# Gated linear attention followed by a multiplicative FFN: first part's output made transposed, heads joined through DRAM, decays moved to partitions by small transfers

## The chip, the cores and the metric

The kernel runs on one core of one Trainium2 chip. The time is the device time of one execution, in microseconds (us). Beside it stands the span of a profiled execution, which is about 2 us shorter (1.7 to 2.1 in every execution on record), and the mean clock that the throttle granted TensorE. All runs compared here were fast (granted clock 0.92 to 0.96) except one execution that is named where it occurs. One execution of each kernel was profiled, and executions of one kernel differ: those of the kernel before had spans of 675.3 to 680.7 us, and its profile, at 675.4, is one of the quickest. So a difference of a few microseconds between two profiles is not a finding by itself. A ratio is the mean time of one kernel's fast runs over the mean time of the kernel before's fast runs in the same rounds, with a 95% interval; it is therefore not quite the ratio of the medians that are quoted beside it.

## The reference, cut to what matters

```python
# q, k, v, alpha: (4 batches, 8 heads, 768 positions, 48), alpha in 0.8..1.0
for t in range(S):                       # part 1, gated linear attention
    state = alpha[:, :, t, :, None] * state + einsum('bhd,bhe->bhde', k[:, :, t], v[:, :, t])
    y[:, :, t] = einsum('bhd,bhde->bhe', q[:, :, t], state)
x = y.transpose(0, 2, 1, 3).reshape(3072, 384)       # the seam: heads side by side
h = (x @ w1) * (x @ w2) @ w3             # part 2; w1, w2: 384x1024, w3: 1024x1024
out = h @ w_out                          # w_out: 1024x384; the weights come in float64
```

## The kernel before

Part 1 runs in 24 chunks of 128 positions, six to a batch. With l the running sum of log(alpha) counted from the middle of the chunk, k is multiplied by e^-l and q by e^l; the state from one chunk to the next is multiplied by e^(sum of this chunk's second half) times e^(sum of the next chunk's first half). Both factors are needed with the feature on the partition. Before, eight matmuls a chunk (`halves`) make them in that layout.

The weights arrive as raw 64-bit words and are turned into float32 tile by tile (36 tiles) by VectorE, ScalarE and GpSimd. Since part 2 multiplies by w3 @ w_out, all of w3 must be converted and folded before part 2 can finish; and the program puts part 2's pieces between part 1's steps from chunk 9 on. So there are two stages: a first one in which weights are converted beside chunks 0 to 8, and a second one that begins with the first *gate* (the 12 matmuls named `pg`).

```python
def decays(n):
    la = las[n % 2]                                  # log(alpha), padded to 64 columns a head
    nc.scalar.activation(la[:, :, 0:D], st.pop(("a", n)), AF.Ln)
    nc.tensor.matmul(lc[:, 0:DM], csum, la[:, :, 0:D], ...)          # 384 columns
    for j in range(NP):                              # the state's factors: 4 products, 2 columns
        nc.tensor.matmul(lc[:, DM + 2*j:DM + 2*j + 2], la[:, 2*j:2*j + 2, :], halves, ...)
    nc.scalar.activation(e[:, DM:], lc, AF.Exp)
    nc.scalar.activation(e[:, 0:DM], lc[:, 0:DM], AF.Exp, scale=-1.0)
    nc.vector.tensor_mul(qks[n % 2][:, :, :, 0:D], st.pop(("kq", n)), e[:, 0:2*DM]...)
...
def attend(n):                                       # y has positions on partitions
    for j in range(NP):
        nc.tensor.matmul(y[:, 2*j:2*j + 2, :], qkT[:, 1, j, :], Ts[n % 2][:, j], ...)
    for h in range(H):
        nc.tensor.matmul(y[:, h, :], ms[:, h % 2, h // 2, :], vc[:, h, :], ...)
    nc.scalar.copy(x, y.rearrange("p h d -> p (h d)"))

def seam(n):                                         # features to partitions, by transposes
    for kk in range(KM):
        nc.tensor.transpose(tp[:, kk, :], x[:, ds(kk*C, C)], ident)
    nc.vector.tensor_copy(out=st["xT", g][:, :, ds(c*C, C)], in_=tp)
    if c == G - 1:
        queue_ffn(g)                                 # part 2 of three chunks
...
for n in range(N):                                   # between(): one weight task, and from
    load(n + AHEAD); transposed(n); between(n)       # chunk 9 on one task of part 2
    scores(n); decays(n + 1); between(n)
    outer(n); between(n)
    attend(n); advance(n); between(n)
    seam(n); between(n)
```

A program's float32 matmul shows as two instructions in the profile, so eight `halves` are four calls here, and sixteen instructions of `y` are eight calls.

## Time and profile before

| | before |
|---|---|
| time, median | 678.39 us (3 runs), 679.19 us (4 runs with those beside the changed kernel) |
| span of the profiled execution | 675.4 us |
| first weight conversion on VectorE starts | 26.18 us |
| first gate starts on TensorE | 192.41 us |
| from there to the end | 483.0 us |

The prediction below shows the shares of the engines. Two more views matter for what followed. The first is the start, in order of time (start, duration, engine or its queue, line, what; SPq is the queue of SyncE):

```profile
2.73 0.71 SPq L101 DMA_DIRECT2D vc<-in_v_dram  x1
3.48 0.93 SPq L98 DMA_DIRECT2D ac<-in_alpha_dram  x1
...
14.48 1.78 SPq L114 DMA_DIRECT2D raw<-in_moe_w_dram  x3
...
14.86 0.96 DVE L198 TENSOR_TENSOR qk<-kq,e 128x768 f32<-128x768 f32 x1 [0.22 <-DMA kq<-in_k_dram]
...
25.24 0.95 DVE L198 TENSOR_TENSOR qk<-kq,e 128x768 f32<-128x768 f32 x1
...
26.18 0.42 DVE L120 TENSOR_SCALAR mant<-raw 128x512 uint32<-128x512 uint32 x1
...
192.41 0.81 PE L315 MATMUL pg<-xT,w 128*128 128x384 f32 x2
```

SyncE goes straight from chunk 0's last load to chunk 1's first (3.48 us) and reaches the first raw weights at 14.48. VectorE, which takes its work in order, has the products of chunks 1 and 2 (14.86 and 25.24) *ahead* of the first conversion at 26.18. The raw words were there by about 21 us (issued from 14.48 on, 4.5 us to landing at the median), so the first conversion did not wait for them; in VectorE's order it stands behind chunk 2.

The second is the cost of the exponentials and of the product that uses them (line, engine, operation, shapes, count | busy us, mean ns | idle before, and what ended it):

```profile
L198 DVE TENSOR_TENSOR qk<-kq,e 128x768 f32<-128x768 f32 x24 | 23.6, 983 | 9.6 <-ACT e L196 9.1 <-DMA kq<-in_k_dram 0.2
...
L196 ACT ACTIVATE e<-lc 128x384 f32<-128x384 f32 x24 | 11.6, 484 | 0.0
```

Each exponential of 384 columns takes 484 ns, and VectorE's product of 768 columns 983 ns.

### The profile page before, as it was taken

What the parts mean: (1) busy time and instruction counts of PE and PEld (TensorE: products, weight loads), DVE (VectorE), ACT (ScalarE), POOL (GpSimd) and SP (SyncE); (2) the same over time, 40 slices, a digit from 0 to 9 for tenths busy, and PEclk for the clock granted to TensorE, in tenths of its full rate; (3) what the DMA queues carried; (4) which work ended last, traced back from release to release, by engine and by line L of the source; (5) the groups of instructions that cost most, each with busy time, mean ns of one, the idle gap of its engine ahead of it and who ended that gap; (6) DMA issues with size and microseconds to landing.
All of it is one profiled execution on the core that took longest, in us unless ns stands there. A gap on an engine that the chain in (4) does not pass through costs nothing.

```text
span 675.4 us, 7729 instructions
## 1 busy us (share of the span) xinstructions
PE 634.9 (94%) x3096; PEld 431.6 (64%) x3096; DVE 229.4 (34%) x369; ACT 169.9 (25%) x333; POOL 128.9 (19%) x144
## 2 busy tenths in 40 slices
PE   5896686998999999999999999999999999999997
PEld 4775675565766666666666666666666666665554
DVE  4589767698321301312122131121302312110110
ACT  3445555566221112111111121111111101110110
POOL 0376656677200000001000100000000000000000
PEclk9857756897999999999999999999999999999999
DMA  9555556677122112012020210201010000000000
GB/s 192 143 161 160 141 140 177 174 209 174 24 40 42 36 35 59 14 34 71 12 48 23 60 36 13 50 21 36 0 48 1 0 13 24 0 1 23 13 0 35
DMA packets 106596, 41.92 MB, mean 62 GB/s; under 512 B 100800, under 2 KB 100800, under 8 KB 106560
## 3 DMA queue, kind: packets, MB, share of 16 engines
q1 hardware_dynamic: 105024, 36.71, 22.9%
q0 software_dynamic: 1536, 4.72, 1.9%
q8 instruction: 24, 0.39, 0.2%
q14 instruction: 12, 0.10, 0.0%
HBM read 36.70 MB, written 4.72 MB: 61 GB/s over the span
## 4 chain that ended last, share of the span: by engine, by line
PE 70%; issue 16%; DVE 8%; POOL 3%; DMA 1%; ACT 1%; POOLq 0%; DVEq 0%; ACTq 0%
PE pg L315 29%; PE po L325 14%; PE y L266 7%; PE pf L305 4%; PE lc L189 3%; PE sc L220 3%; PE lc L191 3%; PE tp L207 3%; DVE mant L120 3%; POOL w L130 2%; PE y L262 2%; DVE power L129 2%; DVE power L127 1%; DMA raw<-in_moe_w_dram 1%; PE tpx L283 1%
## 5 line engine op out<-in xcount | busy, mean ns | idle before, releaser
L315 PE MATMUL pg<-xT,w 128*128 128x384 f32 x768 | 259.9, 490 | 0.0
L315 PEld LDWEIGHTS pg<-xT,w 128*128 128x128 f32 x768 | 141.5, 190 | 87.6
L325 PE MATMUL po<-w3o,ab 128*128 128x384 f32 x384 | 127.7, 488 | 0.0
L318 DVE TENSOR_TENSOR ab<-a,pg 128x384 f32<-128x384 f32 x64 | 35.5, 555 | 242.0 <-PE pg L315 236.6
L325 PEld LDWEIGHTS po<-w3o,ab 128*128 128x128 f32 x384 | 71.6, 190 | 46.2
L317 ACT COPY a<-pg 128x384 f32<-128x384 f32 x64 | 30.7, 479 | 157.4 <-PE pg L315 157.4
L266 PE MATMUL y<-vc,ms 128*128 128x48 f32 x384 | 57.6, 308 | 13.4 <-DVE ms L223 13.3
L253 POOL TENSOR_TENSOR T<-tmp,dec 64x192 f32<-64x192 f32 x40 | 21.6, 540 | 240.3 <-DVE tmp L241 173.7
L266 PEld LDWEIGHTS y<-vc,ms 128*128 128x128 f32 x384 | 55.6, 226 | 16.4 <-DVE ms L223 14.6
L328 POOL DMA_DIRECT2D out_dram<-o x24 | 13.5, 561 | 251.0 <-ACT o L327 251.0
L124 POOL TENSOR_TENSOR mant<-mant,rest 128x512 f32<-128x512 f32 (+1 forms) x36 | 48.3, 1340 | 22.2 <-ACT mant L121 21.7
L305 PE MATMUL pf<-wo,w3T 128*128 128x384 f32 x128 | 46.4, 517 | 0.4 <-DVE w3T L302 0.4
L327 ACT COPY o<-po 128x384 f32<-128x384 f32 x24 | 11.5, 479 | 122.8 <-PE po L325 122.8
L223 DVE TENSOR_TENSOR ms<-sc,keep 128x512 int32<-128x512 int32 x48 | 31.1, 683 | 32.8 <-PE sc L220 32.8
L130 POOL TENSOR_TENSOR w<-mant,power 128x512 f32<-128x512 f32 x28 | 37.1, 1325 | 19.9 <-DVE power L129 19.2
L284 DVE COPY xT<-tpx 128x384 f32<-128x384 f32 x24 | 13.3, 555 | 69.7 <-PE tpx L283 66.4
L305 PEld LDWEIGHTS pf<-wo,w3T 128*128 128x128 f32 x128 | 25.3, 204 | 17.6 <-issue 3.1
L189 PE MATMUL lc<-la,csum 128*128 128x384 f32 x48 | 27.2, 656 | 9.9 <-DVE csum L165 5.6
L120 DVE TENSOR_SCALAR mant<-raw 128x512 uint32<-128x512 uint32 (+1 forms) x36 | 33.2, 923 | 6.8 <-POOL w L130 6.3
L220 PEld LDWEIGHTS sc<-qkT 48*128 48x128 f32 x384 | 25.9, 201 | 12.3 <-issue 9.8
L220 PE MATMUL sc<-qkT 48*128 48x128 f32 x384 | 31.3, 301 | 1.9 <-DVE qkT L211 1.1
L207 PEld LDWEIGHTS tp<-ident,qk 128*128 128x128 f32 x192 | 27.7, 167 | 7.9 <-issue 5.1
(50 smaller groups left out, 492.3 us busy)
## 6 DMA issues: line engine op xcount, KB each, us to landing
raw<-in_moe_w_dram SPq DMA_DIRECT2D x28, 512.0 KB, 4.5
ac<-in_alpha_dram SPq DMA_DIRECT2D x24, 192.0 KB, 3.7
kq<-in_k_dram SPq DMA_DIRECT2D x24, 192.0 KB, 3.6
kq<-in_q_dram SPq DMA_DIRECT2D x24, 192.0 KB, 3.5
vc<-in_v_dram SPq DMA_DIRECT2D x24, 192.0 KB, 2.9
out_dram<-o POOLq DMA_DIRECT2D x24, 192.0 KB, 2.2
raw<-in_moe_w_out_dram SPq DMA_DIRECT2D x8, 384.0 KB, 3.1
```

The lines of the kernel that those rows point to most:

```text
L120: nc.vector.tensor_scalar(top, high, 0x000FFFFF, 0x00100000, op0=ALU.bitwise_and, op1=ALU.bitwise_or)
L124: nc.gpsimd.tensor_add(mant, mant, rest)
L130: nc.gpsimd.tensor_mul(dst, mant, power.bitcast(FP32))
L189: nc.tensor.matmul(lc[:, 0:DM], csum, la[:, :, 0:D], start=True, stop=False, skip_group_check=True)
L207: nc.tensor.transpose(tp[:, j, :], qk[:, i, 2 * j:2 * j + 2, :], ident)
L220: nc.tensor.matmul(sc[i][:, j, :], qkT[r, 0, j, :], qkT[r, 1, j, :], start=True, stop=True)
L223: nc.vector.tensor_tensor(ms[:, i].bitcast(I32), sc[i].bitcast(I32), keep_bc, op=ALU.bitwise_and)
L266: nc.tensor.matmul(y[:, h, :], ms[:, h % 2, h // 2, :], vc[:, h, :], start=first, stop=(h == H - 1), skip_group_check=True)
L305: nc.tensor.matmul(po, w3T[:, j, :], wo[:, j, :], start=(j == 0), stop=(j == KF - 1))
L315: nc.tensor.matmul(p, w[:, kk, ds(f * C, C)], xT[:, kk, :], start=(kk == 0), stop=(kk == KM - 1))
L318: nc.vector.tensor_mul(st["ab", g][:, f, :], a, pb)
L325: nc.tensor.matmul(po, ab[:, f, ds(c * C, C)], w3o[:, f, :], start=(f == 0), stop=(f == KF - 1))
```

## The change

It has three parts. (a) Part 1's output is produced with features on partitions, so that no transposes are needed; v and the state become the stationary operand (the one that is loaded into the array as weights), padded to 64 columns a head. As the padding would remain between the heads, x goes to a DRAM scratch and comes back without it. (b) The `halves` matmuls go. The factors are read out of rows of e, which is on chip already, by transfers that scatter a row over the partitions in pieces of 16 bytes (four values, one of each head pair), from ScalarE's queue, up to four a chunk. To let these rows be read in such pieces, e is laid out with the head pair innermost, so ScalarE writes it and VectorE reads it with a stride of 16 bytes. (c) The exponent at row 0 lacks alpha's first row, so the first rows of all chunks are collected once, at the start, by 32 transfers of 288 single values each (`a0`).

```diff
 # constants, ahead of the loads of chunks 1 and 2
+    with nc.allow_non_contiguous_dma(reason="single values to partitions"):
+        for b in range(B):
+            first = alpha[b].rearrange("(j i) (c s) d -> i d c j s", i=2, s=C)
+            for i in range(2):
+                for j in range(NP):
+                    nc.sync.dma_start(out=a0[ds(DP * i, D), b, :, j], in_=first[i, :, :, j, 0])
     for n in range(1, AHEAD):
         load(n)
 # decays
-        for j in range(NP):
-            nc.tensor.matmul(lc[:, DM + 2 * j:DM + 2 * j + 2], la[:, 2 * j:2 * j + 2, :], halves, ...)
-        e = work.tile([C, 2 * DM + 2 * NP], FP32, name="e", bufs=3)
-        nc.scalar.activation(e[:, DM:], lc, AF.Exp)
-        nc.scalar.activation(e[:, 0:DM], lc[:, 0:DM], AF.Exp, scale=-1.0)
+        e = work.tile([C, 2, 2, D, NP], FP32, name="e")
+        for m, sign in enumerate((-1.0, 1.0)):
+            nc.scalar.activation(e[:, m].rearrange("p i d j -> p j i d"),
+                                 lc.rearrange("p (j i d) -> p j i d", i=2, d=D), AF.Exp, scale=sign)
+            ...
+                for i in range(2):
+                    nc.scalar.dma_start(out=decs[n % 3][ds(DP * i, D), m, :], in_=e[ds(row, 1), i0, i])
-        nc.vector.tensor_mul(...)                    # one product of 768 columns
+        for m in range(2):
+            nc.vector.tensor_mul(...)                # two of 384, reading e with its stride
 # advance
-        nc.vector.tensor_mul(dec, mh[0][:, :, 1:2], mh[1][:, :, 0:1])
+        nc.gpsimd.tensor_mul(dec, decs[(n + 1) % 3][:, 0, :], a0[:, b, c, :])
+        nc.gpsimd.tensor_mul(dec, dec, decs[n % 3][:, 1, :])
 # attend
-                nc.tensor.matmul(y[:, 2 * j:2 * j + 2, :], qkT[:, 1, j, :], Ts[n % 2][:, j], ...)
-            nc.tensor.matmul(y[:, h, :], ms[:, h % 2, h // 2, :], vc[:, h, :], ...)
+                nc.tensor.matmul(y[:, j, :], Ts[n % 2][:, j].rearrange("p i d -> p (i d)"), qkT[:, 1, j, :], ...)
+                nc.tensor.matmul(y[ds(DP * i, DP), j, :], vc[:, 2 * j + i, :], ms[:, i, j, :], ...)
+        for i in range(2):
+            nc.scalar.dma_start(out=to[i, :, :, ds(c * C, C)], in_=x[ds(DP * i, D)])
 # seam: three transposes and a copy a chunk go
+        nc.sync.dma_start(out=st["xT", g], in_=st.pop(("xd", g)).rearrange("(k p) t -> p k t", p=C))
```

## The prediction

> **What bounds the kernel now.** I read the busy shares first (TensorE 94%, VectorE 34%), then the 40 slices:
>
> ```profile
> PE   5896686998999999999999999999999999999997
> DVE  4589767698321301312122131121302312110110
> PEclk9857756897999999999999999999999999999999
> DMA  9555556677122112012020210201010000000000
> ```
>
> A slice is 17 us. There are two stages. For ten slices (170 us) TensorE has gaps and a granted clock of about 0.75, while VectorE and the DMA engines are busy; then TensorE is full at full clock to the end. The table of stretches gives both in numbers (columns: TensorE, weight loads, VectorE, ScalarE, GpSimd, clock, DMA share, GB/s):
>
> ```profile
> 0.00:170.00 170.00, 134.34 (x723) 105.04 (x724) 127.33 (x186) 89.23 (x164) 100.25 (x93) 0.75 0.65 166
> 170.00:676.00 506.00, 500.55 (x2375) 326.52 (x2373) 102.06 (x183) 80.63 (x169) 28.69 (x52) 1.00 0.11 27
> ```
>
> So in the second stage each TensorE microsecond counts in full. TensorE's last wait (3.04 us, for a converted w3 tile) ends at 160.9 us; after it lie three folds of w3, chunks 9 to 23 of part 1 and all of part 2.
>
> The first stage is the weight conversion: 36 tiles, the first at 26.2 us, the last two at 168.7 (VectorE) and 171 us (GpSimd), about 4 us a tile. VectorE is busy 127 of 145 us there, partly because it is held up by GpSimd. The same VectorE instruction, twice:
>
> ```profile
> 155.32 0.42 DVE L127 TENSOR_SCALAR power<-raw 128x512 uint32<-128x512 uint32 x1
> 159.64 1.49 DVE L127 TENSOR_SCALAR power<-raw 128x512 uint32<-128x512 uint32 x1
> ```
>
> It takes 0.42 us beside an idle GpSimd and 1.49 us while GpSimd adds (159.51 to 160.84). The two engines nearly take turns.
>
> Last, one chunk in TensorE's order of time, second stage (start, duration, line):
>
> ```profile
> 223.68 1.16 PE L220 MATMUL sc<-qkT 48*128 48x128 f32 x16
> 224.77 0.91 PE L189 MATMUL lc<-la,csum 128*128 128x384 f32 x2
> 225.52 0.95 PE L191 MATMUL lc<-halves,la 128*128 128x2 f32 x8
> 226.33 4.12 PE L315 MATMUL pg<-xT,w 128*128 128x384 f32 x12
> 230.38 0.67 PE L233 MATMUL s<-vc,qk 128*64 128x48 f32 x16
> 230.98 4.14 PE L315 MATMUL pg<-xT,w 128*128 128x384 f32 x12
> 234.95 1.03 PE L262 MATMUL y<-T,qkT 128*128 128x96 f32 x8
> 235.82 1.91 PE L266 MATMUL y<-vc,ms 128*128 128x48 f32 x16
> 237.56 5.39 PE L325 MATMUL po<-w3o,ab 128*128 128x384 f32 x16
> 242.79 0.49 PE L283 MATMUL tpx<-ident,x 128*128 128x128 f32 x3
> 243.12 5.33 PE L325 MATMUL po<-w3o,ab 128*128 128x384 f32 x16
> ```
>
> Matmuls overlap at their ends, so I count from start to next start: sc 1.09, lc 0.75, halves 0.81, s 0.60, state product 0.87, y 1.74, tpx 0.33, eight transposes tp 0.88 (248.28 to 249.16): 7.07 us a chunk. A gate of 12 matmuls is 4.05, 338 ns each, 0.88 ns a column.
>
> **What the Trainium skill says.** "TensorE: Matmul & The Clock Gate", section LDWEIGHTS: loading time goes by the stationary operand's columns (columns/1.2 ns, so 107 ns for 128), not by what is streamed. The trace agrees: halves streams 2 columns yet takes 0.81/8 = 101 ns, and y with 48 columns 1.74/16 = 109 ns. Both are pure weight loading.
> "TensorEngine Tiling (Array Packing)", Key Properties: different tiles of the array can load and multiply in parallel. The trace agrees in part: s has 64-column weights in two halves of the array and takes 37.5 ns an instruction, under the 48 x 0.88 = 42 of its streaming alone; sc in two row halves takes 68 ns where 128 columns in full would take 113.
> "SBUF — State Buffer", section "SBUF: two separate sides": VectorE and GpSimd share a port pair under an exclusive lock. The 0.42 and 1.49 us above agree.
> "DMA: Bandwidth & Descriptors", Specifications: under 512 B a transfer does a read-modify-write and misses line rate. Here a load of 1024 runs of 192 B goes out about every 0.94 us while the DMA is saturated (7.01 to 10.76 us, four loads); over 16 engines that is 15 ns a run. No row of before shows runs of 4 or 16 B.
>
> **The change, part by part.**
>
> (1) Sums for the state on TensorE (halves) vanish: 8 x 101 ns = 0.81 us a chunk.
>
> (2) Output transposed: y now has v as 64-column weights in two column halves and streams 128 columns, 16 instructions as before. Fully parallel it is 57 ns, in turn 113; I take sc's 68: 16 x 68 = 1.09 for 1.74, a gain of 0.65. The state product streams 128 columns, not 96: 113 or the 109 of loading, so 0.90 for 0.87, a loss of 0.03.
>
> (3) The three transposes of the seam vanish: 0.33. lc reads a tile without gaps and may fall from 375 to 338 ns, a gain of 0.07.
>
> Sum 0.81 + 0.65 - 0.03 + 0.33 + 0.07 = 1.83 us a chunk. The instruction order shows part 2 starting at the same place, in chunk 9, so 15 chunks gain on the path: 15 x 1.83 = 27.5 us.
>
> (4) The detour through DRAM: two stores a chunk, one load a group. There is always work of an older group in front of a group's first gate, even for the last one (in before, x of the last chunk is copied at 604.5 us and the last group's first gate starts at 624.0, after three projections), so a few microseconds of transfers are hidden: 0.
>
> (5) ScalarE issues the small transfers, up to six a chunk. Issues cost SyncE 0.33 to 0.43 us when nothing holds them up, so 2 to 2.6 us of ScalarE a chunk. In the second stage (ScalarE busy 16%) a gate's copy comes at most about 1 us late, which the other PSUM tile's 2.03 us of matmuls covers: 1 us in all. In the first stage the conversion's own ScalarE steps lie behind them; from 8 or 9 chunks x 2.4 = 20 us of issues I let a fifth reach the path: 4 us.
>
> (6) VectorE in the first stage loses xT<-tpx (six copies, 3.3 us, and the 9.2 us it stood waiting for them) and dec (0.9 us); qk is split, which costs about 0.13 x 7. Of these 12.5 us I book 10 as gain, as GpSimd, with 2 us more small products, takes up the rest.
>
> (7) New at the start: 32 transfers of 288 single values stand on SyncE's queue after chunk 0's loads and ahead of chunks 1 to 3 and all weights. They start once VectorE has cleared their target (4.5 us) and need at least 32 x 0.43 = 14 us to issue; 18 values per engine at 15 ns would be 0.27 us each, hidden under the issue, but single values may well be slower. Chunk 1's alpha then lands at 22 us instead of 7, the first raw weight (after 12 more loads of 0.94) at about 34. Chunk 0's work fills only part of it. The first conversion moves from 26.2 to about 37: 11 us lost, 25 if a value costs several times as much.
>
> Sum: 675.4 - 27.5 + 1 + 4 - 10 + 11 = 653.9 us of span; the time lies 3.0 above the span (678.4 against 675.4): 657. TensorE's gains in the first nine chunks, at half clock, also stand on its chain of waits (y alone 13% of the first 175 us); I allow 2 us for them and say **655 us**.
>
> **Rivals.** First, the start becomes the bound: single values at several times 15 ns give 675 or more. For it speaks that SyncE's queue is in order, against it that issue, not data, seems to be the cost of small transfers. Second, the two column halves don't overlap: y stays at 1.8 us, the gain falls to 1.1 us a chunk, and the time is 666. The 37.5 ns of s speak against it, weakly. Third, ScalarE becomes the first stage's bound through its issues, since its busy 89 of 170 us don't count them: 10 to 15 us more, 667. Fourth, the first stage gains more than I book (lc, y and tpx all stand on its chain), giving 640.
>
> **Range and chances.** The second stage's gain is between 16 and 30 us, the first stage's net between -12 and +20. That makes 638 to 674. Faster by over 2% means under 664.8: all rivals but the fourth end above it, the central sum is 10 below. 0.74 faster, 0.23 within 2%, 0.03 slower.
>
> **What would show it.** In the profile after: no halves, no tpx; y near 68 ns an instruction start to start (57 to 113 decides the second rival); a full TensorE row from about slice 10 or 11; SyncE's 32 issues ending near 19 us and the first conversion near 37 us (later: the first rival); VectorE no longer waiting for tpx, and ScalarE's waits in the conversion (the third). I am wrong if the full stage begins much later than 175 us or if gates begin to wait for ScalarE's copies.

## The result, and the profile after

The changed kernel is correct. It took 672.21 us (median of 4 runs, 669.35 to 672.87) against 679.19 for the kernel before; the ratio is 0.9887 [0.9855, 0.9919]. That is 1.1% less: within the predicted range, but not the 3.5% less of its central figure, nor the more than 2% that it held most likely.

The busy shares in 40 slices of the changed kernel (a slice is 16.8 us) and its two stretches, with the columns that the prediction explains:

```profile
PE   3472535498799999999999999999999999999997
...
DVE  3159776877842330231222213303303222110110
```

```profile
0.00:170.00 170.00, 94.31 (x535) 65.41 (x536) 112.22 (x157) 83.56 (x144) 90.23 (x95) 0.76 0.67 161
170.00:671.00 501.00, 491.44 (x2300) 306.98 (x2298) 118.82 (x192) 104.93 (x190) 49.23 (x93) 0.99 0.20 48
```

TensorE is as full as before in the second stage, but in the first 170 us it executes 535 matmul instructions where before it executed 723; some of that difference is the removed ones. VectorE has done 112 us of work in the same window, not 127. To see whether there is more work or later work, one has to count up to the first gate of each kernel: VectorE is then busy for 135 us against 133 before, GpSimd for 109 against 103, ScalarE for 102 against 95 (its transfer issues not counted). That is 2 to 8 us an engine for a gate that is 21.5 us later (below), so most of the delay is work that comes *later*. The first two slices of VectorE (3, 1 against 4, 5) show it.

One chunk in TensorE's order, second stage, to be laid beside that of the prediction:

```profile
242.92 1.16 PE L232 MATMUL sc<-qkT 48*128 48x128 f32 x16
244.01 0.91 PE L195 MATMUL lc<-la,csum 128*128 128x384 f32 x2
244.76 4.03 PE L327 MATMUL pg<-xT,w 128*128 128x384 f32 x12
248.72 0.67 PE L245 MATMUL s<-v,qk 128*64 128x48 f32 x16
249.33 4.14 PE L327 MATMUL pg<-xT,w 128*128 128x384 f32 x12
253.30 1.05 PE L277 MATMUL y<-qkT,T 128*128 128x128 f32 x8
254.28 1.09 PE L281 MATMUL y<-ms,v 128*64 128x128 f32 x16
255.31 0.91 PE L337 MATMUL po<-w3o,ab 128*128 128x384 f32 x2
```

From start to next start: sc 1.09, lc 0.75, s 0.61, state product 0.98, y 1.03, that is 64 ns an instruction. Against the kernel before a chunk gains 0.81 (halves) + 0.71 (y) - 0.11 (state product) + 0.33 (transposes) = 1.74 us, over 15 chunks 26.1 us. From the first gate to the end the profile has 456.6 us where before it had 483.0: 26.4 us less. The second stage gave what was promised.

The start and the first gate, as they were shown of the kernel before:

```profile
4.31 17.83 SPq L181 DMA_DIRECT2D a<-in_alpha_dram  x32
...
12.42 1.23 ACTq L207 DMA_DIRECT2D dec<-e  x2
13.70 0.58 ACT L221 COPY qkT<-tp 128x512 f32<-128x512 f32 x1 [5.76 <-issue]
...
22.18 0.46 SPq L99 DMA_DIRECT2D ac<-in_alpha_dram  x1
...
29.59 1.61 DVE L210 TENSOR_TENSOR qk<-kq,e 128x384 f32<-128x384 f32 x2 [11.86 <-ACT e L199]
...
35.47 6.35 SPq L115 DMA_DIRECT2D raw<-in_moe_w_dram  x3
...
38.74 1.62 DVE L210 TENSOR_TENSOR qk<-kq,e 128x384 f32<-128x384 f32 x2 [1.22 <-ACT e L199]
...
45.40 0.42 DVE L121 TENSOR_SCALAR mant<-raw 128x512 uint32<-128x512 uint32 x1
...
213.88 4.04 PE L327 MATMUL pg<-xT,w 128*128 128x384 f32 x12
```

The 32 transfers hold SyncE's queue from 4.31 to 22.14 us. Chunk 1's alpha goes out at 22.18, 18.7 us later than before. Everything behind it moves: chunk 1's product from 14.86 to 29.59, chunk 2's from 25.24 to 38.74, the raw weights from 14.48 to 35.47, the first conversion from 26.18 to 45.40 (19.2 us later), the first gate from 192.41 to 213.88 (21.5 us later). From the first conversion to the first gate it is 166.2 us before and 168.5 after: the conversion stage itself is hardly longer, it starts later. The line of the `qkT` copy shows a second effect: ScalarE stood 5.76 us, as its first small transfer was not issued before 12.42, 4.5 us after the exponentials. (The profile names one of the 32 transfers as what the copy waited for.)

The account closes: first gate +21.5, rest -26.4, sum -4.9 us, and the spans are 675.4 and 670.5. The medians differ by 7.0 us, 2.1 more, as the profiled execution of the kernel before is a quick one and that of the changed kernel is not.

The same two groups as before:

```profile
L210 DVE TENSOR_TENSOR qk<-kq,e 128x384 f32<-128x384 f32 x48 | 45.2, 984 | 23.1 <-ACT e L199 23.1
L199 ACT ACTIVATE e<-lc 128x384 f32<-128x384 f32 x48 | 37.7, 885 | 48.9 <-PE lc L195 48.9
```

The exponential over 384 columns now takes 885 ns instead of 484, and VectorE's product over 384 columns as long as the one over 768 did. The cause that suggests itself is the 16-byte stride, which an experiment below takes away; the prediction had only 0.13 us a chunk for "qk is split".

### The profile page after: what moved, and what is told of

Its sections match the earlier page's. It is cut to its first block, busy times and chain, and to the rows that moved or that the text cites. A ratio compares the mean times of both kernels' runs of the same rounds, so it can differ in the third digit from the quotient of the medians.

```text
span 670.5 us, 7537 instructions
## 1 busy us (share of the span) xinstructions
PE 585.8 (87%) x2832; PEld 372.4 (56%) x2832; DVE 231.0 (34%) x348; ACT 188.5 (28%) x333; POOL 139.5 (21%) x188
## 3 DMA queue, kind: packets, MB, share of 16 engines
q1 hardware_dynamic: 117952, 41.47, 26.4%
## 4 chain that ended last, share of the span: by engine, by line
PE 62%; issue 17%; DVE 7%; POOL 5%; DMA 4%; ACT 3%; ACTq 0%; SPq 0%; POOLq 0%; DVEq 0%
PE pg L327 28%; PE po L337 14%; PE pf L317 4%; DVE mant L121 3%; PE sc L232 3%; PE y L281 3%; POOL w L131 3%; PE tp L219 2%; PE lc L195 2%; PE y L277 2%; DMA a<-in_alpha_dram 2%; PE s L245 2%; DVE power L130 2%; DMA dec<-e 1%; DVE power L128 1%
## 5 line engine op out<-in xcount | busy, mean ns | idle before, releaser
L330 DVE TENSOR_TENSOR ab<-a,pg 128x384 f32<-128x384 f32 x64 | 35.5, 554 | 249.4 <-PE pg L327 239.0
L232 PE MATMUL sc<-qkT 48*128 48x128 f32 x384 | 34.4, 324 | 24.2 <-ACT qkT L221 19.3
L261 POOL TENSOR_TENSOR dec<-dec,a 128x4 f32<-128x4 f32 x20 | 5.1, 255 | 237.2 <-DMA dec<-e 206.2
L210 DVE TENSOR_TENSOR qk<-kq,e 128x384 f32<-128x384 f32 x48 | 45.2, 984 | 23.1 <-ACT e L199 23.1
L199 ACT ACTIVATE e<-lc 128x384 f32<-128x384 f32 x48 | 37.7, 885 | 48.9 <-PE lc L195 48.9
L232 PEld LDWEIGHTS sc<-qkT 48*128 48x128 f32 x384 | 28.7, 221 | 36.0 <-ACT qkT L221 21.4
L219 PE MATMUL tp<-ident,qk 128*128 128x128 f32 x192 | 31.1, 309 | 12.6 <-DVE qk L210 12.6
L223 DVE COPY qkT<-tp 128x512 f32<-128x512 f32 x24 | 16.6, 690 | 65.9 <-PE tp L219 65.9
L281 PE MATMUL y<-ms,v 128*64 128x128 f32 x384 | 33.4, 300 | 6.5 <-DVE ms L235 6.5
L219 PEld LDWEIGHTS tp<-ident,qk 128*128 128x128 f32 x192 | 25.4, 159 | 21.0 <-issue 12.4
```

The costliest lines, as they stand in the source:

```text
L199: nc.scalar.activation(e[:, m].rearrange("p i d j -> p j i d"), lc.rearrange("p (j i d) -> p j i d", i=2, d=D), AF.Exp, scale=sign)
L210: nc.vector.tensor_mul(qks[n % 2][:, m, :, 0:D].rearrange("p (j i) d -> p j i d", i=2), kq[:, m].rearrange("p (j i) d -> p j i d", i=2), e ...
L219: nc.tensor.transpose(tp[:, j, :], qk[:, i, 2 * j:2 * j + 2, :], ident)
L232: nc.tensor.matmul(sc[i][:, j, :], qkT[r, 0, j, :], qkT[r, 1, j, :], start=True, stop=True)
L281: nc.tensor.matmul(y[ds(DP * i, DP), j, :], vc[:, 2 * j + i, :], ms[:, i, j, :], start=(not inter and j == 0), stop=(j == NP - 1), skip_gr ...
L330: nc.vector.tensor_mul(st["ab", g][:, f, :], a, pb)
```

## The experiments

The second stage came out as computed, so all experiments ask one thing: **what makes the first gate 21.5 us later?** The theory after reading the traces had three terms: the block of 32 transfers at the start (T1), the decays' transfers on ScalarE's queue (T2) and the stride of e (T3). The rivals: the start is harmless and the conversion itself is slowed, by contention or for want of buffers (R1); the transfers cost by their single values, not by their number (R2); the cost is the wait until the values land, not the issue (R3). All times are medians of four runs (of the three fast ones for late10_cvt3); the last three columns are read from the profiled execution.

| run | result | time, us | ratio to before | first conversion | first gate | gate to end |
|---|---|---|---|---|---|---|
| before | correct | 678 to 680 | 1 | 26.2 | 192.4 | 483.0 |
| after | correct | 672.21 | 0.9887 [0.9855, 0.9919] | 45.4 | 213.9 | 456.6 |
| no_a0 | wrong | 652.63 | 0.9596 [0.9561, 0.9631] | 25.3 | 195.3 | 456.5 |
| no_a0_no_dec | wrong | 645.62 | 0.9498 [0.9456, 0.9540] | 24.2 | 187.0 | 456.6 |
| no_a0_no_dec_contig_e | wrong | 642.68 | 0.9449 [0.9417, 0.9482] | 22.0 | 183.6 | 456.6 |
| a0_12dmas | correct | 656.15 | 0.9644 [0.9605, 0.9683] | 35.6 | 198.7 | 456.6 |
| tr_only | correct | 660.29 | 0.9724 [0.9691, 0.9757] | 22.6 | 190.3 | 469.1 |
| sc_only | correct | 681.21 | 1.0028 [0.9989, 1.0067] | 46.4 | 211.1 | 470.0 |
| a0_half | wrong | 666.94 | 0.9826 [0.9794, 0.9858] | 41.6 | 208.2 | 456.6 |
| row_mul | correct | 656.61 | 0.9678 [0.9644, 0.9711] | 24.7 | 197.9 | 456.7 |
| late10 | correct | 651.65 | 0.9580 [0.9546, 0.9614] | 30.3 | 193.7 | 456.5 |
| before_cvt3 | correct | 681.39 | 1.0013 [0.9971, 1.0055] | 27.3 | 193.8 | 483.0 |
| after_cvt3 | correct | 666.93 | 0.9804 [0.9769, 0.9838] | 44.8 | 209.8 | 456.6 |
| dec_unread | wrong | 651.52 | 0.9563 [0.9520, 0.9607] | 24.8 | 193.4 | 456.6 |
| late10_decsync | correct | 657.32 | 0.9673 [0.9633, 0.9712] | 32.3 | 199.0 | 456.5 |
| late10_decpool | correct | 663.51 | 0.9757 [0.9702, 0.9811] | 28.9 | 198.9 | 462.5 |
| late10_cvt3 | correct | 649.06 | 0.9548 [0.9501, 0.9595] | – | – | – |

"Wrong" means that a factor was replaced by 1, so the kernel does the same work on the engines minus the suspected part, and its result is not the reference's. The column "gate to end" is the quiet control: in every variant of the full change but one it is 456.5 to 456.7.

### Three parts taken away one after the other

**no_a0** drops the block at the start (T1):

```diff
-    for x in qks + Ts + decs + [a0]: ...memset(x, 0.0)
-    (the 32 transfers into a0)
+    for x in qks + Ts + decs: ...memset(x, 0.0)
+    nc.vector.memset(a0, 1.0)
```

> The 32 transfers of single values at the start are left out and their target set to 1 (a wrong result on purpose); all else as changed. Theory A (the start is the largest loss: the full stage began 19 to 21 us late because the first conversion moved from 26.2 to 45.4 us): the first conversion comes back to about 28 us, the first gate from 213.9 to about 197, and the time falls from 672 to 653-657. Rival (the conversion stage's own pace sets the end of the stage and takes up an earlier start): 665 or more.

```profile
195.31 4.04 PE L322 MATMUL pg<-xT,w 128*128 128x384 f32 x12
```

The first gate came at 195.3 instead of 213.9, 18.6 us earlier, and the time fell by 19.6. The first conversion is back at 25.3. T1 holds and is the largest term. How much of a delay reaches the gate depends on its size, though, as two runs below show.

**no_a0_no_dec** drops the decays' transfers as well (T2):

```diff
-            nc.scalar.dma_start(out=decs[n % 3][ds(DP * i, D), m, :], in_=e[ds(row, 1), i0, i])
+    for x in decs: nc.vector.memset(x, 1.0)          # once, among the constants
```

> Besides the 32 transfers of the start, the small transfers of the decays from ScalarE's queue are left out too (decays set to 1, a wrong result on purpose); the exponentials still write with a stride. Theory B (layout): these issues cost the path at most 4 us, so 650 to 655, that is within 5 us of the run without the start's transfers. Rival C (ScalarE's issues hold up the conversion): 10 us or more below that run, 643 to 646.

The first gate came 8.3 us earlier still (187.0), the time 7.0 lower. That is more than Theory B's 4 to 5 us and less than Rival C's 10: the issues cost twice what was booked.

**no_a0_no_dec_contig_e** writes e without the stride too (T3):

```diff
-        e = work.tile([C, 2, 2, D, NP], FP32, name="e")
+        e = work.tile([C, 2, NP, 2, D], FP32, name="e")
```

> As the run without any small transfers, but the exponentials are written and read without a stride (wrong result on purpose). Theory B: exponentials fall from 885 to about 490 ns, the products qk from 984 to about 490 ns, and VectorE's about 10 us in the conversion stage come back: 6 to 10 us below the run with the stride, about 643. Rival: the stride's time lies beside other work, within 2 us of the strided run.

The first gate came 3.4 us earlier (183.6), the time 2.9 lower. Its groups show the engines' side, to be laid beside those of the changed kernel:

```profile
L200 DVE TENSOR_TENSOR qk<-kq,e 128x384 f32<-128x384 f32 x48 | 33.3, 730 | 8.3 <-ACT e L196 7.0
L196 ACT ACTIVATE e<-lc 128x384 f32<-128x384 f32 x48 | 21.2, 487 | 41.7 <-PE lc L192 41.6
```

The expected 6 to 10 us did not come. The exponentials are back at 487 ns, as expected; the products' mean only falls from 984 to 730. Their median falls from 859 to 557, however: the mean contains the products that took up to 1658 ns during the conversion. 48 exponentials at 885 ns cost ScalarE some 19 us more in the whole execution than at 487 (48 x 0.398), yet only 3.4 us of first gate come back: most of it lies beside other work. This is the point where the Trainium skill could have warned: "SBUF — State Buffer", Specifications, says that SBUF is read and written in 16-byte lines and that at least two accesses to a line are needed for full bandwidth. A stride of 16 bytes gives each line one. This trace agrees, with 885 against 487 ns.

After the three steps the first gate is at 183.6, 8.8 us earlier than before (192.4). So the sum is 18.6 + 8.3 + 3.4 - 8.8 = 21.5. It closes by construction, as the parts were taken away one after the other; in another order the terms could come out differently. Each of these edits also lets the compiler's scheduler order instructions a little differently, so a term is good to some microseconds, not to tenths.

**Why the layout can't simply be undone:** with e contiguous, the row scatter of 16-byte pieces becomes one of single 4-byte values. By the author's account such a kernel did not build, and neither did one that joins the two transfers of a row into one. No log of these builds is kept, and neither ran.

### The same values in fewer transfers

**a0_12dmas** keeps all 9216 values and results, in 12 transfers of 768 instead of 32 of 288:

```diff
+        first = alpha.rearrange("b (j i) (c s) d -> i c d (b j) s", i=2, s=C)
+        for i in range(2):
+            for c in range(NCH):
+                nc.sync.dma_start(out=a0[ds(DP * i, D), c]..., in_=first[i, c, :, :, 0])
```

> A correct kernel: the same 9216 single values at the start in 12 transfers of 768 instead of 32 of 288. If the cost is the issue (0.56 us each in the changed kernel), the block of issues and values ends after about 7 us instead of 17.8, chunk 1's alpha lands 10 us earlier, and the time is about 662. If the cost is the values (17.8 us over 576 values per DMA engine is 31 ns each), the data still take about 17.8 us, chunk 1's alpha lands at about 26 us as before, and the time stays at 670 to 673.

SyncE's queue in this run, and the first load behind the block:

```profile
4.31 7.79 SPq L180 DMA_DIRECT2D a<-in_alpha_dram  x12
12.14 0.80 SPq L99 DMA_DIRECT2D ac<-in_alpha_dram  x1
```

The block is 7.79 us instead of 17.83, the time 656.15, lower than the expected 662: correct, and 2.4% below the kernel after by the medians. Against no_a0 the first conversion comes 10.3 us later, but the first gate only 3.4. So a block of 8 us costs little at the gate and the 10 us more of the 32 transfers cost 15.2; why the first part is absorbed was not tested. The Trainium skill, "DMA: Bandwidth & Descriptors", Rules for kernel authors, tells to coalesce many small transfers into one; this pair of runs agrees and gives it a size, 10 us of queue for 20 transfers fewer. **a0_half** does the converse: the 32 transfers stay, each with half the values (`b, 0:3, j`).

> The changed kernel with all 32 transfers at the start, but each brings half of the values (144 instead of 288; the other half stays at 1, a wrong result on purpose). If the number of transfers costs (issue[...]), the block stays near 17 us and the time within 3 us of 672. If the values cost, the block falls to about 9 to 15 us (the floor is the issue) and the time falls by 5 us or more.

```profile
4.31 15.61 SPq L182 DMA_DIRECT2D a<-in_alpha_dram  x32
```

Half the values took 2.2 us off the block (17.83 to 15.61), fewer transfers for all the values took 10.0 off it. Number outweighs values in the block. But the time fell by 5.3 us, more than the expected 3, and the first gate came 5.7 us earlier: by the block the run sides with the number, by the time with the values. R2 falls as the main cause and stays as a smaller part.

The block can be split further with the trace: the issues last 0.456 us each at the median, 32 x 0.456 = 14.6 us, and 3.2 us of the block are gaps between them. With half the values a transfer lands 2.7 us after its issue instead of 3.6 (medians), and the gaps shrink to 15.61 - 32 x 0.435 = 1.7 us. So the gaps go with the landing; what makes an issue wait for an earlier landing is not shown by any run. ScalarE's first small transfer depends on the block as well, but only in part: it goes out 4.5 us after the exponentials in the changed kernel and 2.1 us after them in no_a0, which has no block.

### Each half of the change alone

**tr_only** is the kernel before with only the transposed output and the DRAM detour (the new `attend` and `seam`, padded v and T); decays still by `halves`. **sc_only** is the converse: the changed kernel with the old `attend` and `seam`.

> Only the transposed output with the join through DRAM; the decays as before, with eight matmuls a chunk; correct. Theory A (the loss is in the decays' half of the change): from the first gate to the end 456.6 + 15 x 0.81 = 469 us; the first gate comes somewhat before that of the kernel before (192.4) as VectorE no longer waits for the seam, at 183 to 190; time 654 to 662. Rival D (the transposed output itself, its copies and stores, slows the first stage): first gate after 195, time 667 or more.

> Only the decays by small transfers; output and seam as before; correct. Theory A: from the first gate to the end 483.0 - 15 x 0.81 = 471 us; the first gate later than before by the start's 17 to 19 us and by the strided exponentials and products, at 208 to 218; time 681 to 691, slower than before. Rival D: the decays' half is neutral or a gain, time 672 or less.

The second stage split as computed: tr_only's gate to end is 469.1, 13.9 us less than before, sc_only's 470.0, 13.0 less. Their sum, 26.9, is the 26.4 of both together within half a microsecond. The DRAM detour is hidden. In the first stage, sc_only's first gate is 18.7 us later than before and tr_only's 2.1 earlier. Tr_only is inside its expected time (654 to 662) with a first gate at the edge of what was expected (183 to 190). So tr_only gains 2.8% alone; sc_only is the same as before (its interval includes 1), not shown to be slower as its expectation had it. Added up, they would give a first gate at 192.4 + 18.7 - 2.1 = 209.0, but with both it is at 213.9; in medians, tr_only is 18.3 us below its before, sc_only 2.7 above, both together 7.0 below, some 9 us worse than the sum. Both put transfers on ScalarE's queue and both shift the instruction order; which of the two makes the 5 to 9 us is not settled.

### Is it the buffers (R1)?

**before_cvt3** and **after_cvt3** give the conversion a third set of buffers (`cvt = pool("cvt", 3)`, and `outp = pool("outp", 1)` to make room).

> The kernel before with three buffers instead of two for the weights' conversion (and one output buffer instead of three, to make room); correct. Theory P (the conversion stage is paced by the time a tile takes through VectorE, ScalarE and GpSimd with two tiles under way, not by VectorE's busy time): the stage shortens by 10 us or more, time 668 or less. Rival V (VectorE and GpSimd taking turns are the pace): within 4 us of 678.

> The changed kernel with three buffers for the conversion (one output buffer): correct. Theory P: as the path now has ScalarE's issues in the tile's way, a third buffer gains more here than in the kernel before: 12 us or more, 660 or less. Rival V: within 4 us of 672.

Before, nothing came of it (1.0013), as Rival V had it. After, it gave 5.3 us, with the first gate 4.1 us earlier: neither the 12 us of Theory P nor the nothing of Rival V. So buffers did not set the pace in the kernel before, and in the changed kernel a third set buys back a part of the loss. R1 is not the main cause: its first half, a harmless start, is refuted by no_a0, and the stage from the first conversion to the first gate is only 2.3 us longer than before (168.5 for 166.2). Contention by itself was not tested.

### Issue or wait (R3)?

**dec_unread** is no_a0 with the decays' transfers still issued, but with constants used in their place:

```diff
-        nc.gpsimd.tensor_mul(dec, decs[(n + 1) % 3][:, 0, :], a0[:, b, c, :])
-        nc.gpsimd.tensor_mul(dec, dec, decs[n % 3][:, 1, :])
+        nc.gpsimd.tensor_mul(dec, a0[:, (b + 1) % B, c, :], a0[:, b, c, :])
+        nc.gpsimd.tensor_mul(dec, dec, a0[:, b, 0, :])
```

> As the run without the start's transfers (652.6), with the small transfers of the decays issued on ScalarE but never read (GpSimd multiplies constants in their place; wrong result on purpose). If ScalarE's issues cost the 7 us by which leaving the transfers out was faster, it stays at 650 to 654. If it is GpSimd's wait for the values to land, it falls to 645 to 648.

The first gate is at 193.4, against 195.3 with the values read and 187.0 with no transfers. So of the 8.3 us some 6.4 stay with the transfers merely issued. The other 1.9 would be the wait for landing, but that is not shown: the medians of the times are 1.1 us apart (651.52 and 652.63) and the intervals overlap. R3 falls as the main cause of T2. The changed kernel's own row for these issues (min/median/max in ns):

```profile
L207 ACTq DMA_DIRECT2D dec<-e x80: 508/572/1271, 12.4 to 567.1; - x80
```

34 of the 80 are issued before the first gate: 34 x 0.572 = 19 us of ScalarE's queue, of which a third to a half reached the path.

### Versions meant to beat both

**late10** keeps all of the change, merges the start's transfers and puts them behind the loads of chunks 1 and 2. The first chunk of a batch needs none, so ten remain:

```diff
     for n in range(1, AHEAD):
         load(n)
+        for c in range(1, NCH):
+            for i in range(2):
+                nc.sync.dma_start(out=a0[ds(DP * i, D), c]..., in_=first[i, c, :, :, 0])
```

> A correct kernel: the start's values in 10 transfers (the first chunk of a batch needs none), placed after the loads of chunks 1 and 2 instead of before them. If it is the delay of chunk 1's loads and of the weights behind the small transfers that costs, the block of 10 (about 6.5 us) now delays the weights by at most 6 us and chunk 1 not at all: first gate 196 to 199, time 652 to 656, at or below the 12 transfers at the front (656.2). If the number alone counts and not the place, it stays at 656.

```profile
11.24 8.16 SPq L182 DMA_DIRECT2D a<-in_alpha_dram  x10
```

It is correct and takes 651.65 us, 4.2% below the kernel before and 3.1% below the kernel after (by the medians). The block lasts 8.16 us, hardly less than the 7.79 of twelve ahead of the loads, but now it delays only the weights: the first conversion is at 30.3 and the first gate at 193.7, 5.0 us earlier than with a0_12dmas. As the blocks are about equally long, that is the place's doing rather than the two transfers fewer. Place and number are both worth something. The gate is even no later than in no_a0 (195.3), which has no such transfers and converts 5 us earlier: within the few microseconds of scatter nothing of the delay is left.

**row_mul** needs no a0 at all: it multiplies row 0 of e by row 0 of alpha on chip, and keeps a small strided copy `er` of just the rows that are scattered, with e contiguous.

```diff
+        er = work.tile([C, 2, D, NP], FP32, name="er")
+        nc.vector.tensor_mul(er[0:1]..., e[0:1, 0], ac[0:1]...)             # one partition
+        nc.scalar.activation(er[96:C]..., lc[96:C]..., AF.Exp)              # 32 partitions
```

> A correct kernel meant to beat both: no transfers at the start, as row 0 of the chunk's exponentials is multiplied by row 0 of alpha on VectorE before it is scattered; exponentials and products without a stride, only the rows that are scattered are written with one. First gate 185 to 191 and 456.6 us from there: 643 to 650. If the transposed layout's stride and the start are not the causes, it stays above 655.

It missed: 656.61, no better than a0_12dmas. By its own expectation, over 655 would speak against the stride and the start as causes; but the edit also adds work, and no_a0 and no_a0_no_dec_contig_e take these two away without adding any. The likely reason, which no run isolates, stands in one row:

```profile
L196 DVE TENSOR_TENSOR er<-e,ac 1x384 f32<-1x384 f32 x20 | 19.6, 979 | 4.9 <-ACT e L194 3.1 <-DMA xd<-x 0.7
```

A strided product on one partition took 979 ns in the mean, as long as the strided one on 128 partitions (984); the medians are 850 and 859. Making the strided piece narrow saved nothing: nine of these products, 10.2 us of VectorE, and ten strided exponentials, 8.7 us of ScalarE, lie ahead of the first gate.

**late10_decsync** and **late10_decpool** take the decays' transfers off ScalarE and issue them from SyncE or GpSimd.

> Correct; as the best so far (10 late transfers, 651.7), with the decays' transfers issued from SyncE instead of ScalarE. If the place in ScalarE's queue costs, 645 to 648, unless SyncE, which must then wait for each chunk's exponentials before it goes on to the next weights, gives it back. If the transfers as such cost, 650 to 653.

> Correct; the decays' transfers issued from GpSimd. If ScalarE's place costs and GpSimd's own issues (0.56 us each for the output's transfers, four a chunk) cost less: 646 to 650. GpSimd is one of the two engines that take turns in the conversion, so 2.2 us a chunk there should cost as much or more: 651 to 660.

Both are worse than late10, by 5.7 and 11.9 us, and worse than any figure expected of them. ScalarE is the cheapest of the three places in this kernel. With GpSimd the time from the first gate to the end also grew, to 462.5. The trace shows where: TensorE needs 451.8 us from the first gate to its last product in both, and what follows that product lasts 10.7 us instead of 4.7. Why the end is longer is open.

**late10_cvt3** adds the third set of conversion buffers to late10.

> Correct; the best so far with three conversion buffers (one output buffer). If the third buffer covers ScalarE's issues in the tile's way, it gains the same 4 to 6 us as in the changed kernel: 646 to 648. If it only helped with the backlog after the late start, nothing: 650 to 653.

Its three fast executions have a median of 649.06 us; the fourth, the profiled one, was slow (888.53 us at a clock of 0.645), so no profile of it is used. Its interval [0.9501, 0.9595] overlaps that of late10; it is not shown to be better.

## Why the prediction was right or wrong

- **Second stage, parts (1) to (3): right.** 26.4 us measured for 27.5. Of the terms, y gave 0.71 for 0.65 (64 ns an instruction for the assumed 68), the state product cost 0.11 for 0.03 (122 ns for 113), and lc gained nothing where 0.07 was booked.
- **Part (4), the DRAM detour at 0: right.** The time after the first gate is 456.6 with and without every other piece, and tr_only, which has the detour, gave its computed 13.9.
- **Second rival, no column overlap: refuted** by the 64 ns; in turn it would have been 113.
- **Part (6), VectorE freed by 10 us:** the rest of the change, with the three costs taken away, brings the first gate 8.8 us forward. The sum fits; that it comes from VectorE's freed time is not shown. Tr_only frees VectorE of the same copies and waits, and brings the gate only 2.1 us forward, but it keeps `halves` and adds two issues a chunk to ScalarE. And 4.2 of the 8.8 are there already at the first conversion (22.0 for 26.2).
- **Part (7), the start: the step that failed.** The prediction put it as "The first conversion moves from 26.2 to about 37: 11 us lost". It was 45.4, and taking the block away gave 18.6 us. The block itself was sized fairly well (17.8 us for "at least" 14); the first raw load went out at 35.5, so its words were there at about 39.5 (4.0 us to landing at the median) where the prediction had 34. That was not what held the first conversion, which follows chunk 2's masking on VectorE (44.79) without a gap. The error is the step after it: 37 is the prediction's landing of the raw words plus 3 us, as if chunk 1's and 2's work could be done during the wait. But their alpha stands behind the same 32 transfers, and in VectorE's order their products stand ahead of the first conversion: 11.7 us from the first raw load's issue to the first conversion before, 9.9 after. In the changed kernel the delay of the queue (18.7 us at chunk 1's alpha) went through nearly whole; a block of 8 us would not have (a0_12dmas). The prediction's own sign of being wrong, a full stage that begins much later than 175 us, came: the first gate is at 213.9. The mechanism was the first rival's; its cause is not single values that are slow, as that rival had it, but their number and who stands behind them.
- **Part (5), ScalarE's issues: mis-sized.** A fifth of 20 us was allowed to reach the path, 4 us; the issues were 19 us in the first nine chunks as reckoned, but 8.3 came back when they were taken away. The third rival named this, with 10 to 15 us; it was worth more than its place in the sum and less than the rival said.
- **A term was missing: the stride of e,** 3.4 us. It stood in the diff.
- **The sum.** Predicted for the first stage +11 + 4 - 10 = +5, measured 18.6 + 8.3 + 3.4 - 8.8 = +21.5: 16.5 us too little. For the second stage 27.5 and 1 of delay predicted, 26.4 measured. That carries 653.9 to 670.5 of span. That the total fits so well is no test of the single terms, as those of the first stage were measured as a sequence that closes by construction. The chance of "within 2%" at 0.23 was too low, because the range allowed up to +20 for the first stage's net while the chances were set as if +5 were its middle by evidence; no row of the profile before gave the cost of a small transfer.
- **Slips that changed little.** The range does not follow from its parts: a second-stage gain of 16 to 30 us and a net of -12 to +20 in the first give 675.4 - 30 - 12 + 3 = 636 to 675.4 - 16 + 20 + 3 = 682 us, not 638 to 674. The 3.0 us from span to time compare a profiled execution with the median of others; within an execution it is 1.7 to 2.1. TensorE's clock in the first stage is 0.75 in the prediction's own table, not half. And what GpSimd does from 159.51 to 160.84 is a product (L130), not an addition.

## What to carry to other kernels

In this kernel a small transfer cost its issue and its place in an in-order queue, so count the transfers and ask who stands behind them: merged to ten and put behind the loads that start the pipeline, the same values cost nothing that these profiles can tell from scatter, instead of 18.6 us. The saving on the engine that was full came back to the microsecond and could be computed from start-to-start times (26.4 us for 26.1). In the stage where several engines take turns it could not: a first conversion 20.1 us later moved the first gate by 18.6 us, one 10.3 us later by only 3.4. So a delay there has to be measured. Look at each new access pattern's stride as well as at its count of elements; a strided operation didn't get cheaper by using fewer partitions.

## What the Trainium skill lacked or had wrong

- "DMA: Bandwidth & Descriptors", section "Issuing engines are not separate DMA queues", calls the sequencer's time to initiate a DMA "usually small relative to the DMA itself". For a single transfer that agrees: 0.456 us an issue on SyncE, 3.1 to 4.1 us from issue to landing. What the sentence leaves out is that issues add up in one in-order queue while landings overlap: 32 of them held SyncE for 17.83 us. On ScalarE an issue took 0.572 us, against 1.8 us to landing. The page's rule to coalesce says nothing of what stands behind such transfers: the next load went out 18.7 us later. It has no time for transfers of single 4-byte values either; here halving the values of 32 transfers took 2.2 us off the block.
- "SBUF — State Buffer", Specifications, has the rule of 16-byte lines, but no size: here float32 at a stride of 16 bytes took ScalarE 885 ns for 487 at 384 columns. Nor does that table say that using fewer partitions doesn't help: on VectorE 979 ns on one partition, 984 on 128 (medians 850 and 859).
- "TensorEngine Tiling (Array Packing)", Key Properties, says that tiles work in parallel, without saying how far in float32: here 128 columns in two column halves took 64 ns an instruction, between the 57 of full overlap and the 113 of none that the prediction worked out.
